# A hand-ordered attention and FFN kernel: one order of steps for each slot, and a prologue made of steps

## The chip, the cores and the metric

The kernel runs on one core of one Trainium2 chip. The metric is the device time of one execution in microseconds (us), as the median of several runs. In the text PE is the matrix engine (TensorE) and PEld its weight loads, DVE is VectorE, ACT is ScalarE, POOL is GpSimd, and SP is SyncE, whose queue issues most of the DMAs. Each engine works through its own instructions strictly in the order in which the program lists them, and semaphores make it wait for the others.

## The reference

Attention in which a query sees only the keys of its own cluster, followed by a gated FFN with a convolution of three taps over the sequence. There are 4 batches, 8 heads, 768 tokens and 64 elements a head, 16 centroids a head; the FFN has 512 inputs and 1024 hidden channels.

```python
q_assign = argmax(q_n @ c_n)              # nearest centroid by cosine, for each query; k_assign likewise
mask   = q_assign[:, None] == k_assign[None, :]
scores = where(mask, q @ k.T / 8, -1e9)
attn   = softmax(scores)
x      = (attn @ v) of all heads side by side        # [4, 768, 512]
h      = maximum(x @ w_in, 0)                        # [4, 768, 1024]
conv   = sum over 3 taps of conv_w[k] * h shifted by one token
out    = (h * sigmoid(conv)) @ w_out                 # [4, 768, 512]
```

## The kernel before, in words

The work is cut into 32 **slots**. A slot is one pair of heads for one half (384) of the queries of one batch; a batch has eight slots, the first four for the first half of the queries and the last four for the second. So the first four slots need all eight heads of the batch 0. Beside the attention of slot t the kernel runs other work of other slots: it prepares head t + 6, and it works on **unit** n = t - 5 of the FFN (two blocks of 128 hidden channels for one half of a batch).

Each piece of work is a **step** with a short name:

- Head steps, for one head. T: six PE transposes of Q and K side by side, four into the PSUM bank `tra` and two into `trb` (line 186). QA and QB: copies of the two banks to SBUF by DVE (L195) and ACT (L193). CQ: a POOL cast to f16 into the `ext` buffer, by way of `c` and two DMAs for later heads (L200 to L205). CV: a POOL cast of V (L208). A: eight small matmuls with the centroids into `trb` (L214). D: a DVE transpose of the similarities (L227). M0 to M6: seven DVE steps that find the best centroid and write it into `pack` (L236 to L254). K: a PE transpose that turns `pack` (L260). B: a DVE copy of the turned rows and a DMA that puts them into `ext` as three extra rows of the contraction, which is how the mask enters the scores (L265, L266). LQ, LK, LV: the loads. Z: zeroing of the unused rows of an `ext` buffer (L501).
- Attention steps. S0 to S5: two score matmuls each (L323). E0 to E5: the exponential on ACT (L335). V0 to V2: the matmuls with V, in groups of twelve, into the bank `avb` (L342). N: the division by the row sums on DVE (L354, L355). X: three PE transposes into `tra` (L365). Y: their copy by DVE (L369).
- FFN steps. I0, I1: four matmuls each into the bank `fp` (L384). R0, R1: the relu into `hpad` (L399). C0, C1: the carry of border columns on POOL. c, a, b: the three taps of the convolution on DVE (L418, L420). H: tanh on ACT (L450). G: the gate on DVE (L454). O0, O1: four output matmuls each into `fp` (L460). F: the copy of `fp` to SBUF and the output DMA (L472). Six of the eight slots of a steady period have O steps (`FOUTS`).
- W: in each slot some weight loads on POOL's queue, or two of the 24 POOL steps that build the tap matrices for the end.

The order of the steps is a list of names, and nothing else reorders them. `token:1` means the step of the slot before, and `token/5` names the head or unit outright.

```python
    for t in range(NT + 1):
        for token in (SLOTS.get(t, SLOT) if t < NT else END).split():
            step(token, t)
```

Slots 0 to 5 and 27 to 31 have lists of their own; slots 6 to 26 share the list `SLOT`; `END` follows the last slot and `START` stands ahead of slot 0. Ahead of `START` stands a fixed prologue (L478 to L532): the loads of Q and K of all eight heads on SP (K of heads 0 and 1 on ACT's queue), the normalised centroids, constants, zeroings and `keep_busy`, matmuls on zeros whose result is not used (L498; 8 there and 9 in `START`). At the end the convolutions of the last units run on PE (p, L436), and the last output tokens are gathered block by block (u, z) and written out (y).

Of the kernel before, what the change touches and what calls it, by code (L numbers as in the profile page):

```python
# [28 lines left out]
END = (
# [4 lines left out]
)  # L34
SLOTS = {
# [4 lines left out]
    ),  # L40
# [43 lines left out]
def kernel(  # L84
# [73 lines left out]
    pack_b = [const.tile([P, 6, J], F16, name=f"pack{i}") for i in range(3)]  # L158
# [22 lines left out]
    def transposes(h, banks=None):  # L181
        ta, tb = banks or (tra[:], trb[:])
        where[h] = (ta, tb)
        for j in range(J):
            to = ta[:, P * j : P * (j + 1)] if j < 4 else tb[:, P * (j - 4) : P * (j - 3)]
            nc.tensor.transpose(to, qk_t[h][:, j].rearrange("p a d -> p (a d)"), id128[:])  # L186
# [71 lines left out]
    def turn(h):  # L258
        pkT = where[h][1].bitcast(F16)[0 : 6 * J, 384 : 384 + P]
        nc.tensor.transpose(pkT, pack_b[h % 3].rearrange("p a j -> p (a j)"), id16[:])  # L260
# [76 lines left out]
    def values(t, us):  # L337
        b, a, pr, h0 = slot(t)
        for u in us:
            hd, jq = u // 3, u % 3  # L340
            for kt in range(J):
                nc.tensor.matmul(  # L342
                    avp[:, u, 0 : D + 1],
                    lhsT=attn[t, hd][:, kt, P * jq : P * (jq + 1)],
                    rhs=v16_b[(h0 + hd) % NE][:, kt, 0 : D + 1],
                    start=(kt == 0),
                    stop=(kt == J - 1),
                    skip_group_check=True,
                )
# [128 lines left out]
    nc.sync.dma_start(cent[:], centroids.rearrange("h c d -> (h c) d"))  # L478
# [11 lines left out]
    nc.vector.memset(cT32[:], 0.0)  # L490
    nc.vector.memset(nrm_c[:], 1.0)
    nc.scalar.activation(nrm_c[:], nrm_c[:], AF.Sqrt)
    nc.vector.tensor_copy(out=id16[:], in_=id128[:])
    nc.vector.memset(zero.bitcast(F32)[:], 0.0)

    def keep_busy(n):
        for i in range(n):
            nc.tensor.matmul(sc[1][:, i % 2, :], lhsT=id16[:], rhs=zero[:], start=True, stop=True)  # L498
# [4 lines left out]
    keep_busy(8)  # L503
    nc.vector.tensor_tensor(out=sq_c[:], in0=cent[:], in1=cent[:], op=ALU.mult)
    nc.vector.tensor_reduce(out=nrm_c[:], in_=sq_c[:], axis=AX.X, op=ALU.add)
    nc.scalar.activation(nrm_c[:], nrm_c[:], AF.Sqrt)
    nc.vector.tensor_scalar(out=nrm_c[:], in0=nrm_c[:], scalar1=1e-6, scalar2=None, op0=ALU.add)
    nc.vector.reciprocal(out=nrm_c[:], in_=nrm_c[:])
    for a in range(2):
        nc.vector.tensor_tensor(out=cn[:, a], in0=cent[:], in1=nrm_c[:].to_broadcast((P, D)), op=ALU.mult)  # L510
    nc.tensor.transpose(fp[:, 0:P], cn.rearrange("p a d -> p (a d)"), id128[:])
    for a in range(2):
        nc.vector.tensor_copy(
            out=cT32[a * D : (a + 1) * D, :, a * C : (a + 1) * C],
            in_=fp[a * D : (a + 1) * D, 0:P].rearrange("p (h c) -> p h c", h=H),
        )
    nc.scalar.activation(scratch[:], nrm_c[:], AF.Exp)
    nc.gpsimd.iota(iota_rev[:], pattern=[[1, C]], base=0, channel_multiplier=0, allow_small_or_imprecise_dtypes=True)
    nc.gpsimd.tensor_scalar(out=iota_rev[:], in0=iota_rev[:], scalar1=-1.0, scalar2=16.0, op0=ALU.mult, op1=ALU.add)
    nc.vector.tensor_copy(out=iota_ps, in_=iota_rev[:])  # L520
    nc.vector.memset(kscale_ps[:, 0], 512.0)
    nc.vector.memset(kscale_ps[:, 1], -256.0)
    for i in range(3):
        nc.gpsimd.memset(pack_b[i][:, 1, :], -256.0)
        nc.gpsimd.memset(pack_b[i][:, 4, :], 1.0)
    for i in range(4):
        zero_rows(i)

    for i in range(NE):
        nc.gpsimd.memset(v16_b[i][:, :, D : D + 1], 1.0)  # L530
    for i in range(NE):
        nc.gpsimd.memset(v16_b[i][:, :, D : D + 1], 1.0)  # L532
    for token in START.split():
        if token[:2] == "k*":
            keep_busy(int(token[2:]))
        else:
            head_step(*token.split("/"))
# [172 lines left out]
```

## Time and profile before

| What | us |
|---|---|
| Median of three runs | 295.4 (294.16 to 296.53) |
| The profiled execution, its own time | 294.19 |
| Its span, from the first to the last instruction | 292.4 |
| PE busy | 261.5 |
| DVE busy | 231.7 |
| ACT busy | 210.9 |
| POOL busy | 93.5 |

The 1.8 us between the execution's own time and its span lie outside the first and the last instruction. Busy time is the union of an engine's instructions; consecutive matmuls overlap in the record, so four score matmuls that are recorded as 0.81 us hold PE for about 0.65. The granted clock of PE is given as a share of full speed. In a list of groups a row gives line, engine, operation, shapes and count, then the busy time and the mean of one in ns, then the engine's idle time ahead of them and who ended it.

### The profile page before, as it was taken

The page shows a single profiled execution, that of the slowest core. Times are in us where ns is not written, and L with a number is a line of the kernel's source. Part 1 is how long each engine was busy: PE and PEld are TensorE (multiplying, and loading weights), DVE is VectorE, ACT ScalarE, POOL GpSimd, SP SyncE. Part 2 cuts the span into 40 slices and gives each one's busy share as a digit, 9 for nine tenths or more (in the row PEclk, how much of TensorE's full clock was granted, in tenths as well). Part 3 has the DMA queues.
Part 4 walks back from the last instruction along what each step waited for, and adds up shares of the span by engine and source line. Part 5 has one row for each costly group of instructions (what it writes and reads, how often), then busy time and mean ns, then how long its engine had stood idle before and what let it go on. Part 6 is the DMA issues. An engine that isn't in the chain of part 4 may idle for free.

```text
span 292.4 us, 7070 instructions
## 1 busy us (share of the span) xinstructions
PE 261.5 (89%) x2616; PEld 159.5 (55%) x2616; DVE 231.7 (79%) x648; ACT 210.9 (72%) x337; POOL 93.5 (32%) x192
## 2 busy tenths in 40 slices
PE   7685869789899998999999989999999899999992
PEld 3332525455566666666666655666665556565450
DVE  4566886666899989998888989998988887867431
ACT  4215434777899889988888898888898997964321
POOL 6627071722442444444444434323220001001000
PEclk9979686999999999999999999999999999999999
DMA  8994605299457455445555454454522100101103
GB/s 156 213 270 98 157 5 120 50 188 201 75 112 161 112 147 144 113 113 145 146 146 146 137 139 110 119 151 136 139 66 66 37 2 10 64 36 39 72 1 143
DMA packets 65816, 32.78 MB, mean 112 GB/s; under 512 B 53491, under 2 KB 62707, under 8 KB 65782
## 3 DMA queue, kind: packets, MB, share of 16 engines
q1 hardware_dynamic: 61544, 29.30, 39.4%
q0 software_dynamic: 2304, 2.10, 5.1%
q10 hardware_dynamic: 1934, 0.94, 1.1%
q8 instruction: 20, 0.33, 0.5%
q14 instruction: 14, 0.11, 0.1%
HBM read 23.11 MB, written 6.29 MB: 101 GB/s over the span
## 4 chain that ended last, share of the span: by engine, by line
PE 74%; DVE 9%; ACT 7%; DMA 5%; issue 2%; POOL 1%; SPq 0%; DVEq 0%; ACTq 0%
PE sc L323 16%; PE fp L384 11%; PE fp L460 11%; PE avb L342 11%; ACT attn L335 5%; PE trb L214 4%; PE tra L186 4%; PE trb L186 3%; PE sc L460 2%; DMA qk_in<-in_q_dram 2%; PE tra L365 2%; DVE x L355 2%; DMA qk_in<-in_k_dram 2%; PE trb L260 2%; PE sc L436 2%
## 5 line engine op out<-in xcount | busy, mean ns | idle before, releaser
L335 ACT ACTIVATE attn<-sc 128x768 f16<-128x768 f32 x192 | 148.7, 817 | 30.3 <-PE sc L323 29.5
L323 PE MATMUL sc<-ext 128*128 128x384 f16 x384 | 86.7, 331 | 5.5 <-ACT attn L335 4.6
L203 POOL CAST c<-qkT 128x768 f16<-128x768 f32 x24 | 31.3, 1306 | 102.0 <-ACT th L450 76.0
L420 DVE SCALAR_TENSOR_TENSOR cnv<-hpad,cwcol,cnv 128x382 f16<-128x382 f16 (+1 forms) x108 | 60.6, 610 | 0.2
L342 PEld LDWEIGHTS <-attn 128*128 128x128 f16 x1152 | 46.3, 99 | 10.2 <-issue 1.2
L342 PE MATMUL avb<-v,attn 128*128 128x65 f16 x1152 | 48.7, 195 | 0.6 <-ACT attn L335 0.6
L323 PEld LDWEIGHTS <-ext 128*128 128x128 f16 x384 | 33.5, 98 | 27.9 <-issue 12.9
L384 PE MATMUL fp<-xT,w_in 128*128 128x384 f16 x220 | 44.6, 325 | 0.4 <-ACT hpad L399 0.4
L460 PE MATMUL fp<-w_out,hg 128*128 128x512 f16 x144 | 37.9, 380 | 0.0
L454 DVE SCALAR_TENSOR_TENSOR hg<-th,hpad 128x764 f16<-128x764 f32 (+2 forms) x33 | 31.1, 944 | 5.8 <-ACT th L450 3.2
L384 PEld LDWEIGHTS <-w_in 128*128 128x128 f16 x256 | 23.2, 97 | 15.1 <-issue 1.2
L460 PEld LDWEIGHTS <-hg 128*128 128x128 f16 x192 | 17.4, 98 | 21.4 <-issue 5.4
L193 ACT ACTIVATE qkT<-trb 128x256 f32<-128x256 f32 x30 | 11.9, 398 | 22.0 <-DVE spk L265 7.7
L399 ACT ACTIVATE hpad<-fp 128x384 f16<-128x384 f32 x51 | 25.2, 495 | 0.6 <-PE fp L384 0.6
L450 ACT ACTIVATE th<-cnv 128x764 f32<-128x764 f16 (+1 forms) x27 | 22.9, 848 | 2.3 <-DVE cnv L420 2.2
L195 DVE COPY qkT<-tra 128x512 f32<-128x512 f32 x30 | 20.4, 680 | 1.0 <-PE tra L186 0.9
L227 DVE STREAM_TRANSPOSE trb<-trb 128x192 f32<-128x192 f32 x30 | 11.9, 398 | 11.5 <-PE trb L214 7.2
L186 PE MATMUL tra<-id,qk_in 128*128 128x128 f32 x120 | 19.7, 290 | 0.6 <-DMA qk_in<-in_k_dram 0.5
L214 PE MATMUL trb<-qkT,cT 128*32 128x192 f32 x240 | 17.0, 356 | 2.9 <-ACT qkT L193 2.0
L208 POOL CAST v<-v_in 128x384 f16<-128x384 f32 x32 | 15.9, 504 | 9.8 <-DMA v_in<-in_v_dram 9.6
L355 DVE TENSOR_TENSOR x<-avb,rec 128x384 f16<-128x384 f32 x32 | 17.8, 558 | 1.1
L418 DVE TENSOR_SCALAR cnv<-hpad,cwcol 128x382 f16<-128x382 f16 (+1 forms) x54 | 16.9, 314 | 1.3 <-ACT hpad L399 1.2
(107 smaller groups left out, 290.9 us busy)
## 6 DMA issues: line engine op xcount, KB each, us to landing
qk_in<-in_q_dram SPq DMA_DIRECT2D x32, 192.0 KB
v_in<-in_v_dram SPq DMA_DIRECT2D x32, 192.0 KB
qk_in<-in_k_dram SPq DMA_DIRECT2D x30, 192.0 KB
out_dram<-o_sb SPq DMA_DIRECT2D x22, 256.0 KB
ext<-c SPq DMA_DIRECT2D x48, 96.0 KB
w_in<-in_moe_w_in_dram POOLq DMA_DIRECT2D x8, 128.0 KB, 3.5
w_out<-in_moe_w_out_dram POOLq DMA_DIRECT2D x8, 128.0 KB, 4.1
out_dram<-o_sb ACTq DMA_DIRECT2D x2, 256.0 KB
```

What stands on the lines that cost most here:

```text
L186: nc.tensor.transpose(to, qk_t[h][:, j].rearrange("p a d -> p (a d)"), id128[:])
L203: nc.gpsimd.tensor_copy(out=c[:], in_=qkT[h][:])
L214: nc.tensor.matmul(sims[32 * j : 32 * (j + 1), :], lhsT=cT32[:, h % H, :], rhs=tokens[:, j], start=True, stop=True, skip_group_check=True,)
L323: nc.tensor.matmul(s[:, i, 0:HS], lhsT=ext_b[h % NE][:, 1, P * (kt + i) : P * (kt + i + 1)], rhs=ext_b[h % NE][:, 0, HS * a : HS * (a + 1) ...
L335: nc.scalar.activation(attn[t, g // 3][:, kt : kt + 2, :], bank_of.pop((t, g))[:, :, 0:HS], AF.Exp, scale=0.125)
L342: nc.tensor.matmul(avp[:, u, 0 : D + 1], lhsT=attn[t, hd][:, kt, P * jq : P * (jq + 1)], rhs=v16_b[(h0 + hd) % NE][:, kt, 0 : D + 1], star ...
L355: nc.vector.tensor_tensor(out=x16[t].rearrange("p jq (hd d) -> p hd jq d", hd=2), in0=avp[:, :, 0:D].rearrange("p (hd jq) d -> p hd jq d", ...
L384: nc.tensor.matmul(bank[:, 0:HS], lhsT=w_in16[:, r, 2 * u + f, :], rhs=xT[:, b % 2, r, HS * a : HS * (a + 1)], start=(r == 0), stop=(r == ...
L399: nc.scalar.activation(to, bank[:, 0:HS], AF.Relu)
L420: nc.vector.scalar_tensor_tensor(out=cnv, in0=src, scalar=w, in1=cnv, op0=ALU.mult, op1=ALU.add)
L454: nc.vector.scalar_tensor_tensor(out=o[:, fs], in0=th_t[n][:, fs, 0:N], scalar=1.0, in1=h[:, fs], op0=ALU.add, op1=ALU.mult)
L460: nc.tensor.matmul(bank[:, 0:Dm], lhsT=hg_b[b][:, fb, P * tq : P * (tq + 1)], rhs=w_out16[:, fb, :], start=(fb == 0), stop=(fb == NFB - 1) ...
```

## The change

The order becomes a full table: `SLOTS` has a list for each slot from -1 (the prologue) to 32 (the end), and `SLOT`, `START` and `END` go. Steps are cut finer and moved.

- T becomes Ta (four transposes) and Tb (two). V0 to V2 become V0 to V5 with six matmuls each, O0 and O1 become O0 to O3 with two each. LD becomes LQ, LK and LV. Every step may lag by 1 to 4 slots.
- The prologue's instructions become steps with an @ (`setup`): the constants, the centroids' normalisation n0 to n5, zeroings z on POOL and zd on DVE, the weight loads wi and wo, the tap matrices tp.
- The centroids' load goes from SP's queue to ACT's, behind the first Sqrt; K of head 0 stays on ACT's queue, behind it, and K of head 1 goes to SP's. The loads of the first eight heads are spread over slots -1 to 1, with V among them.
- Six matmuls of 384 columns on zeros, into the bank `fp`, stand in the place of 17 of 512.
- `pack` is 128 columns wide (36 hold data, 92 are zeroed once by POOL), so K turns 128 columns.
- Slots 26 and 29 have empty lists; their steps stand in the lists of later slots.

The core of the diff:

```diff
-HEAD_STEPS = "T QA QB CQ CV A D M0 M1 M2 M3 M4 M5 M6 K B".split()
+HEAD_STEPS = "Ta Tb QA QB CQ CV A D M0 M1 M2 M3 M4 M5 M6 K B".split()
...
+    -1: (
+        "@n0 @cT @id @id16 @zero @k/4 @k/1 @k/3 @cent @k/0 @k/2 @zd/5 @pk/0 @k/5 @io0 La/0 @n1 @n2 LQ/0 LK/1 @io1 @n3 "
+        "Ta/0 @n4 QA/0 @v/4 Tb/0 QB/0 LQ/1 LQ/2 Tb/1 A/0 QB/1 D/0 M0/0 @z/3 @z/0 M1/0 Ta/1 @v/6 QC/1 A/1 @v/0 LK/2 "
+        "Ta/2 QC/2 @z/2 CQ/0 LV/0 @v/2 M2/0 Tb/2 @z/1 M3/0 D/1 @v/7 LQ/3 M4/0 CQ/1 @v/3 M5/0 LK/3 M0/1 M6/0 @pk/1 "
+        "LV/1 LQ/4 K/0 CV/0 QB/2 M1/1 A/2 M2/1 Ba/0 CQ/2 M3/1 D/2 Ta/3 @pk/2 M4/1 M5/1 M0/2 LV/2 LK/4 @v/8 M6/1 LV/3 "
+        "@hz/2 Tb/3 QA/3 K/1 QB/3 A/3 Ba/1 @v/11"
+    ),
     0: (
+        "S0 E0 @zd/10 M1/2 D/3 M2/2 LV/4 S1 M0/3 LK/5 M3/2 LQ/5 M1/3 @wi/1 LQ/6 Ta/4 E1 M4/2 Tb/4 @v/9 QA/4 M5/2 M2/3 "
+        "M6/2 @zd/6 S2 QB/4 LV/5 S3 K/2 B/2 A/4 LK/6 CQ/3 @v/10 D/4 E2 S4 E3 Ta/5 CV/4 CV/3 @n5 M3/3 E4 @v/1 M0/4 S5 "
+        "M4/3 @wi/3 CV/1"
+    ),
...
     5: (
+        "I0 E2:1 S3:1 S4:1 V0 R0"
+    ),
...
+    10: (
+        "C1 E3:1 I1 K:2 V0:1 QA:1 S4:1 c0:1 S5:1 LV:2 R1 A:1 N:1 LK:1 D:1 I0 E4:1 S0 H:2 V2 LQ:1 R0 c1:1 M0:1 X:1 G:2 "
+        "V0 M1:1 Y:1 M2:1 E5:1 a1:1 O0:1 B:2 O1:1 S1 E0 V5 O2:1 M3:1 V4 V1 CQ:1 c1 C0:3 O3:1 a0:1 S2 E1 M4:1 a1 Ta V3"
+    ),
...
+    32: (
+        "V2 q1/27 H:2 V3 b1:1 F:1 G:2 c/28 p1/27 V4 V1 V5 V0 Y:1 N a0:1 w0/0 c/29 w1/0 X b0:1 p0/27 e1/0 H:1 Y i1/29 "
...
-    pack_b = [const.tile([P, 6, J], F16, name=f"pack{i}") for i in range(3)]
+    pack_b = [const.tile([P, P], F16, name=f"pack{i}") for i in range(3)]
+    pack_v = [x[:, 0 : 6 * J].rearrange("p (a j) -> p a j", a=6) for x in pack_b]
...
     def turn(h):
-        pkT = where[h][1].bitcast(F16)[0 : 6 * J, 384 : 384 + P]
-        nc.tensor.transpose(pkT, pack_b[h % 3].rearrange("p a j -> p (a j)"), id16[:])
+        nc.tensor.transpose(where[h][1].bitcast(F16)[:, 384 : 384 + P], pack_b[h % 3][:], id16[:])
...
+        if name == "cent":
+            nc.scalar.dma_start(cent[:], centroids.rearrange("h c d -> (h c) d"))
...
+        elif name == "k":
+            nc.tensor.matmul(fp[:, P:512], lhsT=id16[:], rhs=zero[:, 0:384], start=True, stop=True)
...
+        elif name == "n0":
+            nc.vector.memset(nrm_c[:], 1.0)
+            nc.scalar.activation(nrm_c[:], nrm_c[:], AF.Sqrt)
...
+        elif name == "pk":
+            nc.gpsimd.memset(pack_b[i][:, 6 * J : P], 0.0)
...
+    for t in range(-1, NT + 1):
+        for token in SLOTS[t].split():
             step(token, t)
```

More of the change, by code (lines that the diff above doesn't have):

```diff
@@ L179, with transposes @@
     qkT, attn, x16, hg_b, hfs, where = {}, {}, {}, {}, {}, {}
[L181 to L184, printed above, removed]
+    def transposes(h, js):
+        ta, tb = where[h] = early.get(h) or (tra[:], trb[:])
+        for j in js:
             to = ta[:, P * j : P * (j + 1)] if j < 4 else tb[:, P * (j - 4) : P * (j - 3)]
@@ L231, in arg @@
         sim = where[h][1][:, 0:192].rearrange("p (j t c) -> p j t c", j=J, t=2)
-        pack = pack_b[h % 3]
+        pack = pack_v[h % 3]
         best = best_ps.rearrange("p j t -> p t j")
@@ L266, in bias_rows @@
         queue.dma_start(ext_b[h % NE][D : D + BR].rearrange("r a s -> r (a s)"), spk[0 : 6 * J, :])
-    early = {0: (tra[:], trb[:]), 1: (sc[0][:, 0, :], sc[0][:, 1, :]), 2: (fp[:], avb[:])}
+    early = {1: (sc[0][:, 0, :], sc[0][:, 1, :]), 2: (fp[:], avb[:])}
     def head_step(name, h):
         h = int(h)
-        if name == "T":
-            transposes(h, early.get(h))
+        if name == "Ta":
+            transposes(h, range(4))
+        elif name == "Tb":
+            transposes(h, range(4, J))
         elif name in ("QA", "QB", "QC", "QD"):
@@ L335, in exps, with values @@
         nc.scalar.activation(attn[t, g // 3][:, kt : kt + 2, :], bank_of.pop((t, g))[:, :, 0:HS], AF.Exp, scale=0.125)
-    def values(t, us):
+    def values(t, u):
         b, a, pr, h0 = slot(t)
[L339 to L349, printed above, removed]
+        hd, jq = u // 3, u % 3
+        for kt in range(J):
+            nc.tensor.matmul(
+                avp[:, u, 0 : D + 1],
+                lhsT=attn[t, hd][:, kt, P * jq : P * (jq + 1)],
+                rhs=v16_b[(h0 + hd) % NE][:, kt, 0 : D + 1],
+                start=(kt == 0),
+                stop=(kt == J - 1),
+                skip_group_check=True,
+            )
     def normalize(t):
@@ L403, in carry @@
         if a == 0:
-            if u == 0:
+            if b not in hfs:
                 hfs[b] = rot.tile([P, NFB, 4], F16, name="hf", tag="hf")
@@ L427, in gated @@
         b, a, u = unit(n)
-        if n % NU == 0:
+        if b not in hg_b:
             hg_b[b] = rot.tile([P, NFB, S], F16, name="hg", tag="hg")
@@ L489 @@
     cn = const.tile([P, 2, D], F32, name="cn")
[L490 to L498, printed above, removed]
     def zero_rows(i, eng=nc.gpsimd):
         eng.memset(ext_b[i].bitcast(F32)[D:P].rearrange("p a s -> p (a s)"), 0.0)
-    keep_busy(8)
@@ L504 @@
[L504 to L537, printed above, removed]
@@ L553, in weights @@
             )
-        for i in (2 * t, 2 * t + 1):
-            if t < 4:
-                r, f = i // 2, slice(NFB // 2 * (i % 2), NFB // 2 * (i % 2 + 1))
-                nc.gpsimd.dma_start(
-                    w_in16[:, r, f].rearrange("p fb f -> p (fb f)"),
-                    moe_w_in[r * P : (r + 1) * P, f.start * P : f.stop * P],
-                )
-            elif t < 8:
-                i -= 8
-                nc.gpsimd.dma_start(w_out16[:, i], moe_w_out[i * P : (i + 1) * P, :])
+        elif name == "wi":
+            r, f = i // 2, slice(NFB // 2 * (i % 2), NFB // 2 * (i % 2 + 1))
+            nc.gpsimd.dma_start(
+                w_in16[:, r, f].rearrange("p fb f -> p (fb f)"),
+                moe_w_in[r * P : (r + 1) * P, f.start * P : f.stop * P],
+            )
+        elif name == "wo":
+            nc.gpsimd.dma_start(w_out16[:, i], moe_w_out[i * P : (i + 1) * P, :])
+        elif name == "tp":
+            fb, kk = i // 3, i % 3
+            nc.gpsimd.tensor_scalar(
+                out=taps16[:, fb, kk, :], in0=id16[:], scalar1=cwcol[:, fb, kk : kk + 1], scalar2=None, op0=ALU.mult
+            )
+        else:
+            raise KeyError(name)
     fouts = {}
@@ L575, in step @@
         name, _, h = token.partition("/")
-        if h and name[0].islower():
+        tt = t - lag
+        if name[0] == "@":
+            setup(name[1:], h)
+        elif h and name[0].islower():
             last_step(name, h)
@@ L580, in step @@
         elif name in HEAD_STEPS:
-            h = t + AHEAD - lag
-            if H <= h < NH:
-                head_step(name, h)
-        elif name == "LD":
-            if H + 2 <= t + AHEAD + 2 < NH:
-                for what in ("Lq", "LV"):
-                    head_step(what, t + AHEAD + 2)
+            if H <= tt + AHEAD < NH:
+                head_step(name, tt + AHEAD)
+        elif name in LOADS:
+            if H + 2 <= tt + AHEAD + 2 < NH:
+                head_step(name, tt + AHEAD + 2)
@@ L604, in step @@
                 if name == "F":
[L605 to L606 removed]
+                    evac(b, tq, fp, on_act=tt < NT - 4)
+                    del fouts[tt]
                 else:
                     i = int(name[1])
[L609 to L623 removed]
+                    ffn_out(b, tq, (2 * i, 2 * i + 1), fp)
+        else:
+            n = tt - LAG
+            if n < 0 or tt >= NT:
@@ L627, in step @@
             elif name[0] == "R":
-                relu(n, int(name[1]), fp, on_dve=name[1] == "1" and t >= NT - 4)
+                relu(n, int(name[1]), fp, on_dve=name[1] == "1" and tt >= NT - 4)
             elif name == "C0" and not unit(n)[1]:
@@ L675, in last_step @@
             raise KeyError(name)
-    for t in range(NT + 1):
-        for token in (SLOTS.get(t, SLOT) if t < NT else END).split():
+    for t in range(-1, NT + 1):
+        for token in SLOTS[t].split():
             step(token, t)
```

205 lines of the change are left out of this document (129 added, 76 removed), and 68 rows, old and new, of tables (END, SLOTS).

## The prediction

> **What bounds the kernel now.** First I read the head of the profile page and its strip of 40 slices, to see where the engines are not full.
>
> ```profile
> span 292.4 us, 7070 instructions
> PE 261.5 (89%) x2616; PEld 159.5 (55%) x2616; DVE 231.7 (79%) x648; ACT 210.9 (72%) x337; POOL 93.5 (32%) x192
> ...
> PE   7685869789899998999999989999999899999992
> ...
> DVE  4566886666899989998888989998988887867431
> ...
> PEclk9979686999999999999999999999999999999999
> ```
>
> PE is full from the tenth slice on. The first nine slices (66 us) are where PE and DVE are both short of full and where the granted clock falls below full speed. Next I cut the span at the places that the code gives: the first score (S0 of slot 0), the first FFN matmul (I0 of unit 0), the start of slot 9, I0 of unit 21 near slot 26, and the last exponential. In the table of windows each engine's busy time is followed by its instruction count in brackets.
>
> ```profile
> 20.25 0.48 PE L323 MATMUL sc<-ext 128*128 128x384 f16 x2 [0.65 <-POOL v L208]
> 66.72 0.81 PE L384 MATMUL fp<-xT,w_in 128*128 128x384 f16 x4
> ...
> core 0: us, PE busy (x) PEld busy (x) DVE busy (x) ACT busy (x) POOL busy (x), PEclk, DMA share, GB/s
> 0.00:5.79 5.79, 3.78 (x9) 1.30 (x10) 1.99 (x11) 3.17 (x5) 4.90 (x42) 1.00 0.68 140
> 5.79:20.25 14.46, 11.01 (x59) 5.90 (x60) 9.39 (x33) 2.42 (x6) 5.56 (x8) 0.88 1.15 235
> 20.25:66.72 46.47, 35.84 (x347) 21.10 (x348) 32.04 (x99) 25.18 (x38) 22.06 (x42) 0.85 0.54 112
> 66.72:93.59 26.87, 24.04 (x289) 15.44 (x288) 24.35 (x72) 23.13 (x38) 9.89 (x18) 1.00 0.67 134
> 93.59:221.19 127.60, 124.70 (x1364) 79.69 (x1362) 117.96 (x343) 112.01 (x184) 47.90 (x75) 1.00 0.49 129
> 221.19:262.41 41.22, 38.45 (x400) 23.80 (x398) 32.74 (x73) 36.20 (x54) 1.70 (x4) 1.00 0.09 33
> 262.41:292.40 29.99, 23.67 (x155) 12.28 (x153) 13.25 (x23) 8.78 (x16) 1.53 (x5) 0.98 0.17 62
> ```
>
> The middle (93.59 to 221.19) is PE at 124.70 of 127.60 us, or 98%: no order can take more than 2.9 us out of it without making PE's work shorter. The **ramp** (20.25 to 66.72) is another thing: DVE, its most loaded engine after a PE slowed to a clock of 0.85, works 32.04 of 46.47 us, 69%. In the ramp eight heads are prepared (two a slot, where later slots prepare one), and each goes PE, ACT, PE, DVE, PE, DVE through one PSUM bank pair. The waits of that stretch show DVE standing behind PE in turn, in small pieces:
>
> ```profile
> DVE pack L250 <- PE trb L214: 2.0, 2, 1.2
> DVE pack L248 <- PE trb L186: 2.0, 2, 1.4
> ```
>
> Here a step of one head (L248, L250) waits for the transposes or assignment matmuls of the next head, because it was written behind a step that needs them: waits made by order, not by data.
>
> **The start.** The change issues the centroid load and K of head 0 on ACT's queue behind the first Sqrt, and 6 keep-busy matmuls of 384 columns stand where 17 of 512 stood.
>
> ```profile
> 0.72 0.39 SPq L478 DMA_DIRECT2D cent<-in_centroids_dram  x1
> 0.72 1.40 ACTq L173 DMA_DIRECT2D qk_in<-in_k_dram  x2
> ...
> 2.16 1.28 ACT L492 ACT_TABLE_LOAD   x1 [2.16 <-issue]
> ...
> 5.79 1.08 PE L186 MATMUL tra<-id,qk_in 128*128 128x128 f32 x4
> ...
> 14.01 0.22 PE L260 MATMUL trb<-id,pack 128*36 128x128 f16 x1 [2.23 <-POOL ext L200]
> 14.65 3.73 PE L498 MATMUL sc<-zero,id 128*128 128x512 f16 x9
> ```
>
> The table load of 1.28 us and the centroid issue of 0.39 now precede K of head 0, so it is issued about 1.7 us later and the first transpose moves from 5.79 to 7.4. Head 0's bias turn came 8.2 us after its first transpose (14.01); A/0 no longer stands behind the six transposes of head 1 (at 1.08 for four, 1.6 us), so K/0 comes near 14.0. PE's new order before S0 is K/0, A/2, Ta/3, Tb/3, K/1, A/3. Between K/0 and K/1 DVE has M1, M2, M3, M0, D, B and three pack steps, 2.5 us by the rows of the next part and some 0.4 of gaps; then follow QA/3 (0.68) and A/3 (0.9, twice its warm 0.46 further down, as the clock may be low). S0 starts near **18.6** (before: 20.25, behind the 3.73 us of keep-busy). Bounds 17 and 21. This alone is worth 1.6 us, and less DVE work is done by then.
>
> Loads: SP's list has LV/0 sixth, where it was behind the Q and K of all eight heads. B/2 on SP now stands ahead of LK/6 and all later loads, which wait for that copy; behind it nothing is late, since at the 235 GB/s of the second window a 192 KB load takes 0.84 us and LK/6 is needed some ten us after. Cost 0; if B/2 slipped by 10 us, LK/6 would be late by as much.
>
> **The ramp.** Counted in both orders from S0 of slot 0 to I0 of unit 0, the new order has on DVE one head less in D, M0 to M6 and B (7 for 8), seven zeroings for six, and the same QA, N and Y.
>
> ```profile
> L195 DVE COPY qkT<-tra 128x512 f32<-128x512 f32 x30 | 20.4, 680 | 1.0 <-PE tra L186 0.9
> L227 DVE STREAM_TRANSPOSE trb<-trb 128x192 f32<-128x192 f32 x30 | 11.9, 398 | 11.5 <-PE trb L214 7.2 <-ACT qkT L193 2.4 <-ACT attn L335 1.5
> L236 DVE TENSOR_REDUCE mx<-trb 128x12 f32<-128x192 f32 x30 | 10.5, 350 | 0.3
> L248 DVE TENSOR_SCALAR pack<-trb 128x12 f16<-128x12 f32 x32 | 5.2, 164 | 3.0 <-PE trb L186 2.0 <-ACT qkT L193 0.5 <-PE trb L260 0.3
> L265 DVE COPY spk<-trb 36x128 f16<-36x128 f16 x30 | 6.2, 208 | 1.1 <-PE trb L260 0.9
> L501 DVE MEMSET ext<- 64x768 f32 x8 | 5.6, 698 | 1.7 <-issue 1.5 <-DVE val L244 0.2
> ```
>
> That head is 0.398 + 4 x 0.350 (M1 to M3 are as wide as M0) + 3 x 0.164 + 0.208 = 2.50 us, so DVE has 32.04 - 2.50 + 0.70 = 30.2 us to do. Written step by step in the new order, its neighbours are M steps of two heads in turn (D/4 M3/3 M0/4 M4/3 M1/4), so that one head's wait for PE is filled with the other's work. What is late next is PE's order: K of a head needs M6, and the next A stands behind that K. The share that DVE reaches is bounded by 69% (as now: 43.8 us) and 100% (30.2 us); the stretch after the ramp has 24.35 of 26.87, 91% (33.2 us). I take **80%**, midway between the two measured ones: 37.8 us, so I0 at 18.6 + 37.8 = 56.4 instead of 66.72, a gain of **10.3 us**.
>
> Part of it is given back: four score steps and four exponentials of slots 4 and 5 and one head now stand behind I0. On PE, by the next rows, a score step is 0.33 (four matmuls take 0.81, two 0.49, so 0.16 each); a head's T is 0.65 (146.42 to 147.07), its A 0.46 at most (0.53 with the pipeline's end in it) and its K 0.25: **+2.7 us** of later PE work. The stretch 66.72 to 93.59 has 2.8 us of idle PE but DVE at 91%, so I don't count on it.
>
> **The middle.** Two intervals, the same score step in slots without and with the output matmuls (O), and the bias turn:
>
> ```profile
> 88.04 0.81 PE L323 MATMUL sc<-ext 128*128 128x384 f16 x4
> 94.90 0.81 PE L323 MATMUL sc<-ext 128*128 128x384 f16 x4
> ...
> 139.38 0.81 PE L323 MATMUL sc<-ext 128*128 128x384 f16 x4
> 141.82 0.49 PE L323 MATMUL sc<-ext 128*128 128x384 f16 x2
> 142.24 0.23 PE L260 MATMUL trb<-id,pack 128*36 128x128 f16 x1
> 142.40 0.53 PE L214 MATMUL trb<-qkT,cT 128*32 128x192 f32 x8
> 144.93 0.33 PE L365 MATMUL tra<-id,x 128*128 128x128 f16 x3
> 145.09 0.81 PE L323 MATMUL sc<-ext 128*128 128x384 f16 x4
> 146.42 0.60 PE L186 MATMUL tra<-id,qk_in 128*128 128x128 f32 x4
> 147.07 0.81 PE L323 MATMUL sc<-ext 128*128 128x384 f16 x4
> ```
>
> A slot takes 6.86 us without O and 7.69 with it; only four of the 17 slots in the middle are without, and the new order lets their neighbours' work flow into them (lags of 1 to 3). That can win from 0 to the 2.9 us of idle PE; I take 1. The turn of 36 columns holds PE from 142.15 (141.82 plus two matmuls at 0.163) to 142.40, 0.25 us, while three x transposes with 128 columns take 0.16 together, 0.055 each. With 128 columns the turn could win from 0 to 0.2 us a head (below 0 there is no reason: the moving side stays 128 columns). The A behind it, with 32 columns in f32, keeps its own start, so I take 0.06 for 17 slots: 1. The three POOL memsets of 92 columns lie on an engine that is 32% busy: 0, and on their way only if CQ waited. Middle: **-2.0**.
>
> The Trainium skill, in "TensorE: Matmul & The Clock Gate", section "Weight-path perf modes — Fast Weight Load (FWL) and DoubleRow", says that the fast weight load is on when the weights are 128 and not FP32; the intervals 0.25 and 0.055 agree with it, and by that rule the whole 0.2 of the turn would go, 3.4 us for the middle in place of 1.
>
> **From 221.19 to the end.** PE has 2.8 us idle up to 262.41 (38.45 of 41.22), exponentials at 36.20 of 41.22 beside it: -1.5 of 0 to -2.8. The last stretch is 29.99 us with 23.67 of PE; it is a chain of relu, conv, tanh, gate and output matmul with the output DMA at its end, and the new list holds the same steps in another order with about the same PE work left at the last exponential: -1, of +2 to -3.
>
> **The sum**, against the profiled execution: 294.2 - 10.3 + 2.7 - 2.0 - 1.5 - 1.0 = 282.1 us. The median of the runs, 295.4, is 1.2 above that execution, so the forecast for a median is **283 us**. A change under 1% (about 3 us) can hardly be told from none here.
>
> **Rivals.** *Chain-bound ramp* (the change doesn't do what it says). If each head's way through PE, ACT and DVE sets the pace, DVE stays at 69%, I0 comes at 62.4 and the time is 289. For it: ACT waits for DVE and PE in the ramp too; against: the waits quoted are of another head's work.
>
> *Half clock* (the slower side). PE's ramp work is 35.84 - 2.7 = 33.1 us at a clock of 0.85. If, with the keep-busy matmuls gone, the clock stays near 0.5 until I0, PE takes 33.1 x 0.85 / 0.5 = 56 us, I0 comes at 75 and the time is 302. It decides once the mean clock falls below 0.56, where PE takes 50 us and the other gains are eaten.
>
> ```profile
> 28.00:36.00 8.00, 6.57 (x51) 3.55 (x50) 6.41 (x16) 4.24 (x7) 1.88 (x4) 0.57 0.70 170
> ```
>
> For it: the clock was 0.57 in this window after PE had idled. Against: a shorter ramp holds the same PE work more densely. The Trainium skill has the rule (same page, "Part 1: The HAM clock gate"): an idle window of about 3.4 us halves the clock, a busy one restores it; the 0.57 agrees.
>
> *Handoffs.* The finer order lacks slack: were one exponential (about 0.7 us) a slot left bare on PE for 24 slots, that adds 17 us: 300. It wins over the gains from 0.5 us a slot.
>
> **Chances.** Forecast (277 to 289) 0.55; better (DVE at 91 to 100% in the ramp, down to 271) 0.09; chain-bound (287 to 292) 0.15; half clock, in part or whole (291 to 302) 0.12; handoffs 0.09. So faster by over 1% 0.79, within 1% 0.09, slower 0.12. The range leaves the whole half clock, most handoffs and the deepest gains out: 271 to 295.
>
> **What would show it.** The first transpose near 7.4, S0 of slot 0 near 18.6, I0 near 56 with DVE at 80% between; the clock above 0.7 there; PE at 97% or more in the middle; the turn at 0.05 to 0.2; the last exponential 29 us before the end. I0 after 64, or middle waits of ACT for scores beyond the present ones, would make it wrong.

## The result, and the profile after

The median after the change is **282.88 us** (four runs, 279.53 to 284.07) against 295.07 before (294.16 to 296.53): a ratio of 0.9545, with a 95% interval of 0.9449 to 0.964. The ratios compare means and leave out the runs in the slower state that this chip sometimes shows, 284.07 here and 296.39 of H0 below among them. The changed kernel measured again in six runs beside the experiments gave 281.57 (279.70 to 283.14), a ratio of 0.9583 (0.9537 to 0.9629). The profiled execution took 282.76, its span 281.0 where it was 292.4. The forecast was 283 in a range of 271 to 295. The total came out as forecast; its terms did not, and the experiments below say which of them.

The head of the page and its strips, of the changed kernel:

```profile
span 281.0 us, 7068 instructions
...
PE 256.6 (91%) x2605; PEld 160.4 (57%) x2605; DVE 233.8 (83%) x648; ACT 211.1 (75%) x337; POOL 85.7 (30%) x183
...
PE   4887695899998999999999989999999999999991
...
DVE  4578785478999999999999989989999898897441
...
PEclk9999999579999999999999999999999999999998
```

PE is full from the ninth slice on, where it was from the tenth, and a new dent has come: slices eight and nine (49 to 63 us), where the granted clock reads 5 and 7. The same cuts as before (first transpose, first score S0, first FFN matmul I0, start of slot 9, the late stretch, the last exponential):

```profile
core 0: us, PE busy (x) PEld busy (x) DVE busy (x) ACT busy (x) POOL busy (x), PEclk, DMA share, GB/s
0.00:6.64 6.64, 2.53 (x8) 1.01 (x8) 3.44 (x16) 1.69 (x3) 3.65 (x17) 1.00 0.77 159
6.64:18.27 11.63, 9.81 (x59) 5.45 (x59) 7.33 (x24) 2.85 (x7) 8.54 (x24) 1.00 1.13 242
18.27:60.58 42.31, 33.28 (x328) 20.99 (x325) 28.94 (x89) 23.30 (x36) 20.32 (x41) 0.88 0.65 129
60.58:90.10 29.52, 27.73 (x317) 17.57 (x315) 27.50 (x80) 26.23 (x44) 10.54 (x20) 1.00 0.56 117
90.10:214.30 124.20, 122.27 (x1348) 78.90 (x1346) 119.37 (x342) 112.09 (x184) 39.73 (x73) 1.00 0.52 133
214.30:251.60 37.30, 37.24 (x401) 23.68 (x400) 33.33 (x78) 35.04 (x54) 2.27 (x7) 1.00 0.11 35
251.60:281.00 29.40, 23.73 (x161) 12.82 (x158) 13.87 (x24) 9.88 (x17) 0.64 (x2) 0.95 0.20 72
```

I0 comes at 60.58 where 56.4 was forecast: DVE worked 28.94 of 42.31 us in the ramp, 68%, the same share as before. What the order lost there it won later: PE is full to 0.06 us in the late stretch. To compare the kernels by work done and not by time of day, the next table gives when the same instructions ran, in the profiled executions: the first score, and the start of the last exponential of slots 8, 9, 25 and 31. A0 is the changed kernel once more; the other names are those of the experiments.

| Kernel | first score | slot 8 | slot 9 | slot 25 | slot 31 | span |
|---|---|---|---|---|---|---|
| before | 20.25 | 94.17 | 101.84 | 221.75 | 261.61 | 292.4 |
| after | 18.27 | 90.06 | 96.94 | 214.26 | 250.84 | 281.0 |
| A0 | 18.39 | 88.23 | 94.93 | 212.25 | 248.83 | 279.0 |
| H0, old order | 18.88 | 92.50 | 100.14 | 218.78 | 258.43 | 289.2 |
| H1, old up to slot 8 | 19.33 | 92.54 | 100.17 | 217.43 | 254.01 | 284.2 |
| H2, new up to slot 8 | 17.32 | 90.32 | 99.98 | 218.88 | 258.53 | 289.3 |

Between the profiles of after and A0, of one and the same kernel, the part up to slot 8 differs by 1.8 us and the rest by 0.2: between these two it is the ramp that varies.

### The profile page after: what moved, and what is told of

Its sections match the earlier page's. It is cut to its first block, busy times and chain, and to the rows that moved or that the text cites. A ratio compares the mean times of both kernels' runs of the same rounds, so it can differ in the third digit from the quotient of the medians.

```text
span 281.0 us, 7068 instructions
## 1 busy us (share of the span) xinstructions
PE 256.6 (91%) x2605; PEld 160.4 (57%) x2605; DVE 233.8 (83%) x648; ACT 211.1 (75%) x337; POOL 85.7 (30%) x183
## 4 chain that ended last, share of the span: by engine, by line
PE 69%; DVE 20%; DMA 4%; ACT 3%; issue 2%; DVEq 0%; ACTq 0%
PE sc L424 18%; PE fp L560 10%; PE fp L484 10%; PE avb L442 9%; DVE cnv L520 5%; PE trb L315 4%; PE tra L287 3%; PE sc L560 3%; PE trb L287 3%; DMA ext<-spk 3%; DVE qkT L296 2%; DMA qk_in<-in_k_dram 2%; PE sc L536 2%; PE tra L465 2%; DVE val L345 2%
## 5 line engine op out<-in xcount | busy, mean ns | idle before, releaser
L424 PE MATMUL sc<-ext 128*128 128x384 f16 x384 | 92.3, 335 | 5.0 <-DMA ext<-spk 3.9
L520 DVE SCALAR_TENSOR_TENSOR cnv<-hpad,cwcol,cnv 128x382 f16<-128x382 f16 (+1 forms) x108 | 64.7, 617 | 0.2
L442 PEld LDWEIGHTS <-attn 128*128 128x128 f16 x1152 | 52.7, 99 | 13.8 <-issue 1.9
L442 PE MATMUL avb<-v,attn 128*128 128x65 f16 x1152 | 57.6, 195 | 0.1
L424 PEld LDWEIGHTS <-ext 128*128 128x128 f16 x384 | 33.2, 99 | 26.6 <-issue 11.4
L560 PE MATMUL fp<-w_out,hg 128*128 128x512 f16 x144 | 39.2, 379 | 0.0
L554 DVE SCALAR_TENSOR_TENSOR hg<-th,hpad 128x764 f16<-128x764 f32 (+2 forms) x33 | 30.2, 925 | 6.9 <-ACT th L550 6.9
L304 POOL CAST c<-qkT 128x768 f16<-128x768 f32 x24 | 21.7, 906 | 43.0 <-issue 16.9
L484 PEld LDWEIGHTS <-w_in 128*128 128x128 f16 x256 | 22.8, 97 | 15.6 <-issue 3.3
L287 PEld LDWEIGHTS tra<-id,qk_in 128*128 128x128 f32 x120 | 15.4, 152 | 5.3 <-issue 2.3
L518 DVE TENSOR_SCALAR cnv<-hpad,cwcol 128x382 f16<-128x382 f16 (+1 forms) x54 | 17.6, 340 | 0.0
```

Source lines behind the costliest of these rows:

```text
L424: nc.tensor.matmul(s[:, i, 0:HS], lhsT=ext_b[h % NE][:, 1, P * (kt + i) : P * (kt + i + 1)], rhs=ext_b[h % NE][:, 0, HS * a : HS * (a + 1) ...
L442: nc.tensor.matmul(avp[:, u, 0 : D + 1], lhsT=attn[t, hd][:, kt, P * jq : P * (jq + 1)], rhs=v16_b[(h0 + hd) % NE][:, kt, 0 : D + 1], star ...
L484: nc.tensor.matmul(bank[:, 0:HS], lhsT=w_in16[:, r, 2 * u + f, :], rhs=xT[:, b % 2, r, HS * a : HS * (a + 1)], start=(r == 0), stop=(r == ...
L520: nc.vector.scalar_tensor_tensor(out=cnv, in0=src, scalar=w, in1=cnv, op0=ALU.mult, op1=ALU.add)
L554: nc.vector.scalar_tensor_tensor(out=o[:, fs], in0=th_t[n][:, fs, 0:N], scalar=1.0, in1=h[:, fs], op0=ALU.add, op1=ALU.mult)
L560: nc.tensor.matmul(bank[:, 0:Dm], lhsT=hg_b[b][:, fb, P * tq : P * (tq + 1)], rhs=w_out16[:, fb, :], start=(fb == 0), stop=(fb == NFB - 1) ...
```

## Experiments: which stretch brought it

**The two orders, cut and joined.** Both orders were written as one flat list with the head or slot of each step spelled out. H0 runs the order of before with the other parts of the change left in (the turn with 128 columns; 17 keep-busy matmuls as in before, but of 384 columns, so that their number counts with the order here). H1 runs the old order up to the last exponential of slot 8 and then what is not yet done, in the new order; H2 the reverse.

```diff
-    for t in range(-1, NT + 1):
-        for token in SLOTS[t].split():
-            step(token, t)
+    for token in ORDER.split():              # S1~3 is step S1 of slot 3
+        token, _, t = token.partition("~")
+        step(token, int(t or 0))
```

> The changed kernel again, as the base for the others. Both theories: 283 us, between 279 and 285, with the spread following the granted clock in the ramp.

> The order of before, written out step by step, in the changed kernel: it keeps the 128-column turn and the 384-column keep-busy matmuls, and takes the finer tokens without reordering them. Theory 1 (the 128-column turn by itself shortens PE in the middle: the turn held PE 0.26 us from the matmul before and 0.16 to the next, after the change 0.18 and 0.07, so about 0.17 less a head, 17 heads in the PE-bound middle): 292 us, 2.8 less than before, and the middle stretch 2.8 us shorter. Theory 2 (the middle's 3.3 us came from the new order): 295 us, the same as before.

> The order of before up to the last exponential of slot 8, then the remaining steps in the new order, all with the 128-column turn. Theory 1 (the gains sit in separate places and add up; 4.1 us stood at that exponential in the two traces): 287 to 288 us. Theory 2 (the new order's later part gains only because the ramp left work ready in another way): 291 to 293 us, no better than the old order with the wide turn.

> The new order up to the last exponential of slot 8, then the remaining steps in the order of before, all with the 128-column turn. Theory 1 (the parts add up): 287 to 288 us, 4.1 from the start and the ramp and 2.8 to 3.3 from the turn. Theory 2 (what the ramp gains is lost again at the seam or in the PE-bound middle): 291 to 293 us.

Measured, beside 293.39 before: A0 281.57; H0 292.28 (291.84 by the eleven runs that its ratio counts), ratio 0.9952 (0.9925 to 0.9980); H1 286.24, 0.9751 (0.9709 to 0.9792); H2 289.54, 0.9864 (0.9821 to 0.9908). So the order does nearly all of it: by medians, with 291.84 for H0, the new order up to slot 8 alone is worth 2.3 us (H2 against H0), the new order from slot 9 on 5.6 (H1 against H0), and both together 10.3 (A0 against H0). H1 came out below either theory's figure, and H2 between the two. H0 has theory 1's 292 us, but not by its account: from slot 8 to slot 25 it is 1.3 us shorter than before (127.58 to 126.28, not 2.8), and 1.7 us of its profile lie ahead of that, 1.4 of them at the first score. The halves do not add up: 2.4 us appear only with both. By the four ratios that difference is no larger than its uncertainty, so the table has to show it. H2 reaches the end of slot 8 as early as after does, but its slot 9 then takes 9.66 us where after's takes 6.88: the new ramp leaves head work undone (13 heads are turned at that point, 14 in before) that the old order of slot 9 pays in one piece. The 20 us around that seam, in the table of windows of H2 and then of after:

```profile
90.00:110.00 20.00, 18.23 (x188) 11.61 (x186) 19.03 (x56) 15.96 (x27) 5.71 (x9) 1.00 0.52 133
```

```profile
90.00:110.00 20.00, 19.92 (x225) 12.89 (x224) 19.73 (x59) 17.77 (x30) 4.94 (x10) 1.00 0.64 165
```

PE stands 1.77 us in H2 and 0.08 in after. A hybrid that cuts an order somewhere charges the seam to one of its halves; the 2.3 for the new order up to slot 8 is therefore a lower figure, and 4.7 (A0 against H1) the one with the seam mended.

**The middle and the late stretch** can be read without a seam. The same 16 slots (last exponential of slot 9 to that of 25), then slots 26 to 31, of before and then of after:

```profile
101.84:221.75 119.91, 117.01 (x1282) 74.84 (x1281) 110.53 (x321) 105.19 (x174) 44.73 (x70) 1.00 0.49 129
221.75:261.61 39.86, 37.09 (x393) 23.12 (x392) 31.75 (x70) 34.84 (x54) 1.70 (x4) 1.00 0.09 34
```

```profile
96.94:214.26 117.32, 115.44 (x1273) 74.53 (x1270) 112.55 (x320) 105.52 (x173) 38.51 (x70) 1.00 0.51 133
214.26:250.84 36.58, 36.52 (x396) 23.33 (x395) 32.61 (x76) 34.32 (x53) 2.27 (x7) 1.00 0.11 36
```

In the middle PE's work falls by 1.57 us and its idle time by 1.02 (2.90 to 1.88). In the late stretch PE's work falls by 0.57 and its idle time by 2.71, from 2.77 to 0.06: nearly all that an order could win there without less PE work.

**The turn alone.** E4 is the changed kernel with the turn of 36 columns put back; the memsets of the other 92 stay.

```diff
-        nc.tensor.transpose(where[h][1].bitcast(F16)[:, 384 : 384 + P], pack_b[h % 3][:], id16[:])
+        nc.tensor.transpose(where[h][1].bitcast(F16)[0 : 6 * J, 384 : 384 + P], pack_b[h % 3][:, 0 : 6 * J], id16[:])
```

> The changed kernel with the turn of the packed rows at 36 columns again (the memsets stay). In the old order the wide turn was worth 1.4 us (292.3 for 293.4 and the ratio 0.995). Theory 1 (PE is the bound nearly everywhere after the ramp in the new order, so each of the about 26 turns behind the ramp costs its 0.17 us): 4 us more than the base, 285 to 286. Theory 2 (as in the old order, only the slots with output matmuls feel it): 1 to 2 us more, 283.

Measured: 282.97 (281.00 to 285.18), 0.9638 (0.9598 to 0.9678), so the 128 columns are worth 1.4 us by medians (A0 281.57). That is theory 2's size, though the intervals of the two ratios overlap, so the time alone does not prove it; the PE work below does. Its window over the same 16 slots, which answers to 115.44 of 117.32 in after:

```profile
95.90:214.90 119.00, 117.41 (x1273) 74.45 (x1270) 113.12 (x320) 106.36 (x173) 38.44 (x70) 1.00 0.51 130
```

It is PE work, 1.97 us for 16 heads or 0.12 each; the stretch itself is 1.68 longer. In the list of times, turn and following matmuls in H0, then the turn between its neighbours in E4 and in after, whose PE lists are the same step by step:

```profile
140.12 0.22 PE L298 MATMUL trb<-id,pack 128*128 128x128 f16 x1
140.27 0.53 PE L253 MATMUL trb<-qkT,cT 128*32 128x192 f32 x8
```

```profile
139.76 0.49 PE L424 MATMUL sc<-ext 128*128 128x384 f16 x2
140.18 0.23 PE L360 MATMUL trb<-id,pack 128*36 128x128 f16 x1
140.34 0.66 PE L287 MATMUL tra<-id,qk_in 128*128 128x128 f32 x4
```

```profile
140.32 0.49 PE L424 MATMUL sc<-ext 128*128 128x384 f16 x2
140.64 0.22 PE L360 MATMUL trb<-id,pack 128*128 128x128 f16 x1
140.70 0.61 PE L287 MATMUL tra<-id,qk_in 128*128 128x128 f32 x4
```

With A behind it the turn of 128 columns holds PE 0.15 us in H0, where that of 36 held it 0.25 in before: 0.1 a head in the same order, as the forecast assumed for an A that keeps a start of its own. In the changed order A follows in only two of the 16 turns. Here it is 0.58 us from the score matmuls to the transposes in E4 and 0.38 in after: 0.2 for one turn, and 0.2 is also the median of all 16. Together these intervals are 2.6 us shorter; 0.9 of that goes again at later matmuls, why is not shown, and 1.7 of the stretch is left. So the rule of the Trainium skill that was weighed in the prediction agrees at the turn itself, with 0.2 a head where A does not follow; the 3.4 us worked out from it did not come, but 1.4 to 1.7.

## Experiments: why the ramp won so little

In the changed kernel the list of PE's waits from 18 to 62 us is led by one wait, and that of DVE's from 18.27 to 60.58 likewise (one list after the other; engine, line and what it waited for; us, times, longest):

```profile
PE sc L424 <- DMA ext<-spk: 3.9, 1, 3.9
```

```profile
DVE qkT L296 <- PE tra L287: 5.2, 2, 4.9
```

PE waits for the rows of head 7 (step B, a copy of 9 KB into `ext`), and DVE for PE. The list of times shows the copy and its company:

```profile
40.44 1.06 POOL L657 DMA_DIRECT2D w_in<-in_moe_w_in_dram  x2
...
42.84 0.79 SPq L366 DMA_DIRECT2D ext<-spk  x1
...
44.08 1.12 POOL L662 DMA_DIRECT2D w_out<-in_moe_w_out_dram  x2
...
46.41 0.54 POOL L662 DMA_DIRECT2D w_out<-in_moe_w_out_dram  x1 [0.34 <-DMA w_in<-in_moe_w_in_dram]
...
50.32 0.80 PE L424 MATMUL sc<-ext 128*128 128x384 f16 x2 [3.95 <-DMA ext<-spk]
```

And the DMA part of the profile for 36 to 52 us (busy share in 40 slices; KB each; median us from issue to landing):

```profile
DMA  0118910001389998998677889999999999999999
...
w_out<-in_moe_w_out_dram POOLq DMA_DIRECT2D x5, 128.0 KB, 7.6
```

Ten weight loads of 128 KB were issued on POOL's queue from 40.44 to 46.41, some of them between the lines shown. Three of the w_out loads stand in the list of slot 6; POOL ran ahead and issued them while slot 3 ran. In before the weight loads had gone out in pairs, twelve of them from 23.94 to 62.2. From 40.4 us on (the twelfth digit) the DMA engines are at six tenths to full, and the 9 KB issued at 42.84 let the score go at 50.32, 7.5 us later. Behind the wait the clock halves (windows of after):

```profile
40.40:50.30 9.90, 5.89 (x76) 3.85 (x75) 5.63 (x17) 4.80 (x8) 7.43 (x14) 0.97 1.05 177
50.30:60.60 10.30, 10.28 (x86) 6.59 (x87) 5.66 (x16) 4.80 (x7) 0.96 (x2) 0.54 0.73 161
```

PE is full for 10.30 us at a clock of 0.54. The lead over before, by the last exponentials, was 10.3 us at slot 2 (41.5 against 51.8) and 3.7 at slot 3 (54.5 against 58.2). Two reasons were open: the rows stand in SP's queue behind loads of heads, or the DMA engines are full whatever the queue. E1 puts the rows of head 7 on ACT's queue; E2 moves the ten weight loads, five to an earlier and five to a later place; E3 does both.

The five w_in loads still to come in slots 3 and 4 go together ahead of CQ/7 in slot 3, the five w_out loads of slots 4 and 6 to the start of slot 8; their old places are left empty. The heart of E1, and then of E2 (each line is a part of a longer one):

```diff
-S0 K/7 LK:1 B/7 E0 S1 Tb:1 CQ/7
+S0 K/7 LK:1 Ba/7 E0 S1 Tb:1 CQ/7
...
-S0 K/7 LK:1 B/7 E0 S1 Tb:1 CQ/7
+S0 K/7 LK:1 B/7 E0 S1 Tb:1 @wi/0 @wi/5 @wi/6 @wi/7 @wi/4 CQ/7
...
-I1 E3:1 R1 A:1
+@wo/0 @wo/1 @wo/2 @wo/3 @wo/5 I1 E3:1 R1 A:1
```

> The changed kernel with one token altered: the bias rows of head 7 go out on ACT's DMA queue instead of SP's, where six loads of later heads stand ahead of them. In three executions of the new ramp PE waited 3.8 to 4.8 us for such rows, and the clock fell to half right behind it. Theory 1 (the rows stand behind the loads in their own queue): the wait of PE for the rows is gone or under 1 us, the clock stays at 1.0 up to the first FFN matmul, and the time falls by 3 to 6 us, to 276 to 278 (base 281.6). Theory 2 (all DMA engines are full of weight and head loads, whatever the queue): the wait stays at 2 us or more and the time falls by less than 2 us.

> The changed kernel with the weight loads of POOL's queue moved: five of w_in ahead of the cast of head 7, five of w_out from slots 4 and 6 to slot 8. The rows of head 7 stay on SP's queue behind the six loads. Theory 1 (order in the queue): the wait shrinks only as far as the loads ahead land sooner, from 3.9 to 1 to 3 us, time 279 to 281. Theory 2 (weight traffic takes the DMA engines): the wait goes nearly whole, the six loads take about half as long each, time 276 to 279.

> Both edits together. If either alone takes the wait away, this one is like the better of the two, 276 to 278; if each takes a part, it is lower than both by 1 to 2 us.

Measured, beside 293.31 before: E1 281.60 (281.06 to 283.82), ratio 0.9589 (0.9561 to 0.9617); **E2 277.86** (277.06 to 279.11), 0.9463 (0.9433 to 0.9493); E3 278.89 (278.19 to 280.86), 0.9505 (0.9474 to 0.9537). E1 brings nothing (A0 281.57), and its list of times says why:

```profile
43.24 0.72 ACTq L366 DMA_DIRECT2D ext<-spk  x1
...
50.82 0.80 PE L424 MATMUL sc<-ext 128*128 128x384 f16 x2 [2.78 <-DMA ext<-spk]
```

On a queue of its own the copy still took until 50.82, 7.6 us after its issue. It was not the queue. The Trainium skill states this in "DMA: Bandwidth & Descriptors", section "Issuing engines are not separate DMA queues": whichever engine issues them, DMAs run on the same 16 DMA engines and interleave; E1 agrees. (The reason with SP's queue was also counted wrongly beforehand: only four loads of heads were issued between the rows of head 6 and those of head 7, at 37.80 and 42.84.) In E2 five loads are gone from the stretch and five are issued from 35.88 on, well ahead of the rows; the list of times and the DMA part read:

```profile
44.62 0.80 SPq L366 DMA_DIRECT2D ext<-spk  x1
...
47.91 0.49 PE L424 MATMUL sc<-ext 128*128 128x384 f16 x2
```

```profile
w_in<-in_moe_w_in_dram POOLq DMA_DIRECT2D x5, 128.0 KB, 5.1
```

The same score goes at 47.91, without a wait on record and in 0.49 us for two matmuls where it took 0.80: 3.3 us after the issue of its rows. The last exponential of slot 3 comes at 50.5 for 54.5 (A0: 54.9), so all of the 3.7 us by which E2's median beats A0's are there at that point. That POOL has less to issue there is not the reason: its casts start at 39.02, 45.40 and 48.61 in E2, no sooner than in after (38.80, 45.24 and 46.93). What is left there in E2 is a wait of 1.7 us for the rows of head 6, the head before, which now go out beside five weight loads. In the table of windows, from S0 to I0, DVE's share in E2 is 74%:

```profile
17.64:54.42 36.78, 29.52 (x323) 19.26 (x324) 27.26 (x87) 22.37 (x36) 17.61 (x35) 0.92 0.62 123
```

So E1 and E2 came out as theory 2 has it. In E3 PE waits for rows 0.8 us in all, and yet it is no faster; the intervals of the two ratios overlap, so it may be no slower either. It was forecast at 276 to 278. ACT, whose queue must now wait for DVE's copy ahead of the issue, shows a new line among its waits:

```profile
ACT attn L436 <- DVE x L455: 1.8, 1, 1.8
```

That this wait is what E3 lost, if it lost anything, is argued and not shown.

## Experiments: the keep-busy matmuls

The changed kernel runs its first transposes at half clock. E5 is E2 with 13 keep-busy matmuls in the place of 6 (three more ahead of n3, four behind it), E6 is E2 with none.

```diff
-... @k/4 @k/1 @k/3 @cent @k/0 @k/2 @zd/5 @pk/0 @k/5 @io0 La/0 @n1 @n2 LQ/0 LK/1 @io1 @n3
+... @k/4 @k/1 @k/3 @cent @k/0 @k/2 @zd/5 @pk/0 @k/5 @io0 La/0 @n1 @n2 LQ/0 LK/1 @io1 @k/6 @k/7 @k/8 @n3 @k/9 @k/10 @k/11 @k/12   # E5
+... @cent @zd/5 @pk/0 @io0 La/0 @n1 @n2 LQ/0 LK/1 @io1 @n3                                                                       # E6
```

> The kernel with the moved weight loads (277.9 us) and seven more keep-busy matmuls of 384 columns around the centroids' transpose, 13 in all. Theory 1 (the half clock of the first 16 to 20 us costs time, and more work early lifts it): the head transposes before the first score run at full clock, 0.6 us for four in place of 1.1, the first score comes 1 to 1.5 us sooner and the time falls by 1 us or more, to 276 to 277. Theory 2 (the chain through DVE and ACT sets the pace there): no change of more than 0.7 us.

> The same kernel without any keep-busy matmuls. Theory 1 (the half clock costs time): the clock rises later than with six, and the time is 1 to 3 us more, 279 to 281. Theory 2: no change of more than 0.7 us, so that the six are as good as none.

Measured, beside 293.64 before: **E5 276.63** (275.88 to 277.59), ratio 0.9420 (0.9395 to 0.9444), faster than both kernels: 5.8% under before, and by the two ratios (0.9420 over 0.9583) 1.7% under the change; E6 278.11 (276.71 to 279.27), 0.9461 (0.9436 to 0.9487), the same as E2 with six. The lists of times and the first window of each, E5 and then E6:

```profile
6.62 0.63 PE L287 MATMUL tra<-id,qk_in 128*128 128x128 f32 x4 [0.31 <-DMA qk_in<-in_k_dram]
...
17.59 1.46 PE L424 MATMUL sc<-ext 128*128 128x384 f16 x4 [2.11 <-DMA ext<-spk]
```

```profile
6.62:17.59 10.97, 5.88 (x59) 3.32 (x59) 9.10 (x31) 3.79 (x7) 9.02 (x25) 0.93 1.19 256
```

```profile
6.54 1.09 PE L287 MATMUL tra<-id,qk_in 128*128 128x128 f32 x4 [1.20 <-DMA qk_in<-in_k_dram]
...
18.17 1.46 PE L424 MATMUL sc<-ext 128*128 128x384 f16 x4
```

```profile
6.54:18.17 11.63, 9.81 (x59) 5.44 (x59) 7.33 (x24) 2.85 (x7) 8.53 (x24) 1.00 1.14 244
```

In E5 four transposes take 0.63 us and in E6 1.09. The first score gains only 0.58 on E6, because in E5 it waits 2.11 us for a copy of rows, at a DMA share of 1.19; on E2's profile (17.64) it gains nothing. So the time is theory 1's, but it did not come by an earlier first score. But DVE has done 9.10 us of its work by then and not 7.33 as in E6, and the last exponential of slot 3 comes at 50.6 and not 52.5. Six of these matmuls are too few to be sure of the clock. In after four transposes still took 1.12 us at 12.02, in E2 0.66 at 11.55; the trace's first record of the clock, at full speed, stands at 10.1 us in E2, E3 and E4, at 15.6 in H2 and at 19.4 to 22.3 in E1, A0 and after (E5: 5.8; E6: 21.3). E2's runs may therefore be a mixture, which would explain the 1.2 us between the medians of E5 and E2; it stays open, since the one profile of E2 is level with E5's at slot 3 (50.5 and 50.6).

## Why the prediction was right, and where it was not

The forecast's terms, measured between the last exponentials of slots 8, 25 and 31 (less than a microsecond from the forecast's cuts); the second figure is A0's where it differs:

| Term | Forecast | Measured |
|---|---|---|
| Up to slot 9 (start, ramp, work given back) | -10.3 + 2.7 = -7.6 | -4.1 (-5.9) |
| Middle (order 1, turn 1) | -2.0 | -3.4 (-3.6) |
| Late stretch | -1.5 | -3.3 |
| End | -1.0 | -0.6 |
| Sum of the profiles | -12.1 | -11.4 (-13.4) |

The total was right because two misses cancel, which is luck: 3.5 us too little up to slot 9 (1.7 in A0), 3.2 too much behind it.

- **The start**: right in the sum, wrong on the way. The first transpose came at 6.64 and not 7.4, S0 at 18.27 (18.6 forecast). The table load did not hold up the loads as assumed; ACT's list of times is quoted under the last heading.
- **The ramp** is the step that failed. DVE was to rise to 80% and stayed at 68%. That the lead was 10.3 us at slot 2, the forecast's very figure, is chance: it stood there at 41.5 us and not at I0 (9.5 in A0), with seven heads turned where before had turned eight. Then the step priced as "Cost 0" broke: it looked at SP's queue, found the head loads early enough, and did not price the ten weight loads on POOL's queue, whose transfers meet the rows of heads 6 and 7. E2 puts the price of that at 3.7 us. With it mended I0 comes at 54.42, and the lead at slot 8 is 94.17 - 84.86 = 9.3 us, above the forecast's 7.6. Even so DVE's share was 74% and not 80. I0 came early because 27.26 us of DVE work stood ahead of it, where the forecast counted 30.2 (28.94 in after); no run here separates what holds DVE at 74%.
- **The work given back**: I0 to slot 9 grew from 26.87 to 29.52 us, 2.65 for 2.7, but not as the forecast had it. PE's work grew by 3.69 us (24.04 to 27.73) and its idle time fell by 1.04, on which the forecast did not count.
- **The turn**: 0.2 a head at the turn in the changed order, the upper bound, and 0.1 in the old one (H0); 0.12 a head is left in PE's work over the stretch (E4). 0.06 was taken. Median 1.4 for 1.0.
- **The middle's order**: 1.02 us of idle PE removed in slots 10 to 25, for the forecast 1. Slot 9 gave another 0.8 (7.67 to 6.88), but as less PE work, not less idle time: PE was busy 7.67 us of it in before and 6.83 in after.
- **The late stretch** is the term that was mis-sized the other way: 1.5 was taken midway between 0 and the 2.8 us of idle PE, and 2.71 went. H1 against H0 shows it as the order's own work: 36.58 for 39.65 us.
- **The end**: 29.99 to 29.40 us by the windows, with 23.73 us of PE work in it for 23.67. PE still stands a fifth of the time.
- **Chain-bound ramp** (289) came true in its sign, 68%. The weight loads explain a part of it (74% in E2), a reason other than a head's own way through the engines; whether that way holds the rest is open. **Half clock** showed from 50.3 to 60.6 at 0.54; the mean of 0.88 stayed far above the 0.56 from which it decides. **Handoffs** did not show: in the middle PE works 122.27 of 124.20 us.

## What to carry to other kernels

Count the bytes in flight where a small copy is on the critical path: a 9 KB copy that a matmul waited for took 7.5 us beside ten weight loads that nobody needed yet; another queue did not help it, and moving the bulk loads did. A step's place in an order of names does not say when an engine that has nothing to wait for will run it: loads listed in slot 6 went out while slot 3 ran. When a finer order is priced, the bound of each stretch is PE's idle time in it. In the late stretch, with ACT busy 87% and DVE 80% beforehand, nearly all of it was won (2.71 of 2.77 us), not half; in slots 10 to 25, with DVE at 92%, it was 1.02 of 2.90. When two halves of an order are tested apart, look at the seam before reading the difference as the worth of a half.

## What the runs showed of the hardware that was not expected

**A DMA issue passes a table load.** On ACT the program lists the first Sqrt ahead of the loads of the centroids and of K. ACT's list of times in after:

```profile
0.72 1.28 ACT L601 ACT_TABLE_LOAD   x1 [0.72 <-PEq L789]
0.90 0.40 ACTq L588 DMA_DIRECT2D cent<-in_centroids_dram  x1
1.33 0.68 ACTq L275 DMA_DIRECT2D qk_in<-in_k_dram  x1
2.02 0.20 ACT L601 ACTIVATE nrm_c<-nrm_c 128x1 f32<-128x1 f32 x1
```

The two DMAs were issued at 0.90 and 1.33, while the load ran from 0.72 to 2.00 and the Sqrt itself started at 2.02. So an engine's list is not kept to strictly where it issues DMAs, or the compiled list differs from the program's, which the trace does not show. The first transpose was 0.8 us earlier than worked out.

**The clock column says 1.00 where PE ran at half speed.** In 6.64 to 18.27 it reads 1.00, and yet:

```profile
6.64 1.09 PE L287 MATMUL tra<-id,qk_in 128*128 128x128 f32 x4 [1.11 <-DMA qk_in<-in_k_dram]
...
18.27 1.46 PE L424 MATMUL sc<-ext 128*128 128x384 f16 x4
```

The same four transposes take 0.63 in E5, and four score matmuls 0.81 once warm. The trace's first record of the clock is at 22.3 us; ahead of it the column says nothing, and durations do.

**A half clock can outlast a busy stretch.** PE was busy 10.28 of 10.30 us from 50.3 on and the record of the clock is at half from 49.6 to 59.8 (10.2 us; also in H2 and E1); in A0 and E4 the same wait cost 3.4 us of half clock. What decides between the two lengths no run here shows.
